# Fixed owners for two double banks of scores and maxima products in an attention and expert kernel

## The chip, the cores and the metric

The kernel runs on one core of one Trainium2 chip. The metric is the device time of one execution in microseconds (us), lower is better. TensorE multiplies matrices into PSUM, a small accumulation memory of eight banks of 2 KB per partition; VectorE, ScalarE and GpSimd work beside it, and SyncE issues transfers. In profiles they are called PE, DVE, ACT, POOL and SP.

## The reference, cut to what matters

Three layers follow each other. Attention comes first, for 2 batches of 8 heads, 768 positions and head size 64. Each query and each key gets a hash bucket of 6 bits, and a query sees only keys of its own bucket. Then comes a dense gated layer, then a layer of 8 experts with one expert per token.

```
mask = q_bucket[:, :, :, None] == k_bucket[:, :, None, :]
scores = scale * np.matmul(q, k.transpose(0, 1, 3, 2))
scores = np.where(mask, scores, -1000000000.0)
scores = scores - np.max(scores, axis=-1, keepdims=True)
attn = np.exp(scores)
attn = attn / (np.sum(attn, axis=-1, keepdims=True) + 1e-09)
attn_out = np.matmul(attn, v)
# dense layer
a = x @ w1;  b = x @ w2;  h = a * b @ w3;  x = h @ w_out
# experts
e_idx = np.argmax(x @ w_gate + modality_bias[modality_id], axis=1)
out[mask] = gate_w[mask, None] * (np.maximum(x[mask] @ w1[e], 0.0) @ w2[e])
```

## The kernel before, in words

Attention runs over eight head pairs of 768 positions. The work is cut into units, twelve for a pair. A **maxima** unit (`stage_1`, L336) multiplies 128 queries of one head with all 768 keys, two matmuls of 384 columns (L341) into a double bank of PSUM; VectorE then takes the row maxima straight from there (L348, `tensor_reduce` into `nm`). After six units GpSimd and a transpose (`stage_f`, L357) turn the maxima into two extra rows of the query operand. A **scores** unit (`stage_2`, L369) multiplies 128 keys of both heads with 384 queries, four matmuls (L376) into a double bank; ScalarE takes the exponential from there into `pt` (L377), and GpSimd or, for one unit in six late on, VectorE adds the `pt` tiles up (L383). `stage_a` (L385) multiplies `pt` with the values (L391).

A loop over slots (L777) puts the units in order. Slot i issues maxima unit i (for i below 96 = `NU`) and scores unit i - 9 (for i from 9 = `LEAD` to 104). So slots 0 to 8 hold maxima only, 9 to 95 both, maxima first and scores last on TensorE, and 96 to 104 scores only. Names in the trace and the order tell the unit: `m7_4_1` is head pair 7, query tile 4, head 1, which is slot 93; `s7_0_0` of the same slot is pair 7, half 0, key tile 0. Below, "the reduction of slot 93" is that of its maxima, "the exponential of slot 93" that of its scores.

Between these units other work fills the slots. Pieces of the dense layer's weights are loaded and split into a high and a low part: until slot 86 (`SWITCH`) a piece takes three VectorE operations, a cast on ScalarE (L489) and a difference on GpSimd (L490); later the reloaded first weights take a cast on ScalarE (L489) and a difference on VectorE (L490), queued at the end of a slot (`flush`, L519), so behind that slot's exponential on ScalarE and behind its reduction on VectorE. Products of two weight matrices (L591) fill TensorE from slot 22 on. From slot 90 the input of the dense layer is split too (L633 cast, L635 difference), and from slot 95 the first products of that layer begin (`moe_half`, L669, matmuls L677). After attention the dense layer and the experts follow, TensorE almost without a pause.

Each engine works through its instructions in the order in which they are written; semaphores between engines are put in when the program is built. PSUM tiles come from a pool by a tag (`ps`, L195). The tags `m`, `w`, `u` and `a` have one bank each. The tag `s` has two double banks, and maxima and scores both ask for it. When a tile is asked for, the pool decides at build time which of the tag's two double banks it gets; the tile's first write then waits for the last reader of what lay there. That reader is VectorE's reduction if the bank held maxima, and ScalarE's exponential if it held scores.

Of the kernel before, what the change touches and what calls it, by code (L numbers as in the profile page):

```python
# [20 lines left out]
P = 128  # L21
# [19 lines left out]
LEAD = 9  # L41
# [122 lines left out]
def body(tc, qT, kT, vP, w1d, w2d, w3d, wod, mod, wgate, mbias, e1, e2, cst, out):  # L164
# [25 lines left out]

    pst = ExitStack()
    psum = [pst.enter_context(tc.tile_pool(name="psum1", bufs=1, space=PSUM))]
    nbuf = {"s": 2, "m": 1}

    def ps(tag, shape, name):  # L195
        return psum[0].tile(shape, F32, tag=tag, name=name, bufs=nbuf.get(tag, 1))
# [31 lines left out]
    NU = 2 * 6 * NPAIR  # L228
# [107 lines left out]
    def stage_1(u):  # L336
        p, qt, hd = u
        q, k = head_t[p, hd, "q"], head_t[p, hd, "k"]
        s = ps("s", [P, 2, 512], f"m{p}_{qt}_{hd}")
        for half in range(2):  # L340
            PE.matmul(  # L341
                s[:, half, 0:HS], q[0:KROWS[hd], 0, qt * P:qt * P + P], k[0:KROWS[hd], 0, half * HS:half * HS + HS],
                start=True, stop=True,
            )
        if qt % 3 == 0 and hd == 0:
            nm_t[p, qt // 3] = r_nm([P, 32])
        nm = nm_t[p, qt // 3]
        DVE.tensor_reduce(nm[:, 3 * hd + qt % 3:3 * hd + qt % 3 + 1], s[:, :, 0:HS], AX.XY, ALU.max, negate=True)  # L348
        if qt % 3 == 2 and hd == 1:
            v, fin = nm[:, 6:12], nm[:, 12:24].bitcast(F32R).rearrange("p (d x t) -> p d x t", d=2, x=2)  # L350
            v3 = v.rearrange("p (d t) -> p d t", d=2)
            POOL.tensor_scalar(v, nm[:, 0:6], C_MASK / 2, None, ALU.is_lt)
            POOL.tensor_mul(v, v, nm[:, 0:6])
            POOL.tensor_copy(fin[:, :, 0, :], v3)
            POOL.tensor_sub(fin[:, :, 1, :], v3, fin[:, :, 0, :].bitcast(F32))
# [12 lines left out]

    def stage_2(j):  # L369
        p, half, c = sunits[j]  # L370
        s = ps("s", [P, 2, 512], f"s{p}_{half}_{c}")
        cl = slice(half * HS, half * HS + HS)
        for hd in range(2):
            q, k = head_t[p, hd, "q"], head_t[p, hd, "k"]
            for i, n in enumerate((KROWS[hd], P)):
                PE.matmul(s[:, hd, 0:HS], k[0:n, i, c * P:c * P + P], q[0:n, i, cl], start=(i == 0), stop=(i == 1))  # L376
        ACT.activation(pts[j % NP][:, :, 0:HS], s[:, :, 0:HS], AF.Exp, scale=SCALE)  # L377
        if c == 1:
            acc_t[p, half] = r_acc([P, 2, HS + 1])
        if c:  # L380
            acc = acc_t[p, half]
            on_dve = c in next(cs_ for end, cs_ in ACC_DVE if j < end)
            (DVE if on_dve else POOL).tensor_add(acc, pts[(j - 1) % NP] if c == 1 else acc, pts[j % NP])  # L383
# [174 lines left out]
    slot = [0]  # L558
# [218 lines left out]
    for i in range(NU + LEAD + NLAG + 1):  # L777
# [46 lines left out]
        p, ph = divmod(i, 12)  # L824
# [3 lines left out]
        if i < NU:  # L828
            if p and ph == 9 and p + 3 < NPAIR:
                load_pair(p + 3)  # L830
            stage_1(units[i])
            fill()
            if long:
                fill()
# [30 lines left out]
        if 0 <= j < NU:  # L865
            if j % 12 == 3 and j // 12 + 1 < NPAIR:
                load_v(j // 12 + 1)
            if i == LEAD:
                busy(4, "m")
            stage_2(j)  # L870
            if not both:
                fill()
# [84 lines left out]
    nbuf = {"t": 2, "ab": 4}  # L957
# [582 lines left out]
```

## Time and profile before

| | us |
|---|---|
| median of 3 runs | 686.03 (685.93 to 688.89) |
| the profiled execution, its own time | 685.69 |
| span of that execution | 683.9 |
| TensorE busy | 651.8 (95%) |
| VectorE busy | 386.3 (56%) |
| ScalarE busy | 314.0 (46%) |
| GpSimd busy | 317.8 (46%) |

Busy shares are means over the whole span. Attention fills the first 300 us or so, and there VectorE and GpSimd are loaded heavily in places; from 300 to 600 us TensorE alone is close to 100%. TensorE's granted clock is the full one in nearly all of the span (mean 0.998). The difference between the span and the execution's own time is 1.8 us. A wait in the trace is idle time of an engine, put down to the instruction that ended it.

### The profile page before, as it was taken

The page shows a single profiled execution, that of the slowest core. Times are in us where ns is not written, and L with a number is a line of the kernel's source. Part 1 is how long each engine was busy: PE and PEld are TensorE (multiplying, and loading weights), DVE is VectorE, ACT ScalarE, POOL GpSimd, SP SyncE. Part 2 cuts the span into 40 slices and gives each one's busy share as a digit, 9 for nine tenths or more (in the row PEclk, how much of TensorE's full clock was granted, in tenths as well). Part 3 has the DMA queues.
Part 4 walks back from the last instruction along what each step waited for, and adds up shares of the span by engine and source line. Part 5 has one row for each costly group of instructions (what it writes and reads, how often), then busy time and mean ns, then how long its engine had stood idle before and what let it go on. Part 6 is the DMA issues. An engine that isn't in the chain of part 4 may idle for free. (4 is left out here: it accounts for less than half of the span.)

```text
span 683.9 us, 11034 instructions
## 1 busy us (share of the span) xinstructions
PE 651.8 (95%) x4038; PEld 511.9 (75%) x4038; DVE 386.3 (56%) x617; ACT 314.0 (46%) x534; POOL 317.8 (46%) x312
## 2 busy tenths in 40 slices
PE   7888999999999997999999999999999999999995
PEld 2544566666566754678989898989888899899984
DVE  6897676767586889642632121121275865575550
ACT  7264665556556556553422121221224665564551
POOL 7498888687858776552524233231214212111110
PEclk9999999999999999999999999999999999999999
DMA  8755555473736463303201010100036977766630
GB/s 225 239 187 171 186 150 199 120 234 112 223 111 205 137 203 108 105 20 96 65 16 47 16 47 16 47 1 32 1 121 221 333 267 238 238 205 212 209 115 19
DMA packets 41691, 94.04 MB, mean 138 GB/s; under 512 B 6352, under 2 KB 12032, under 8 KB 41632
## 3 DMA queue, kind: packets, MB, share of 16 engines
q1 hardware_dynamic: 39552, 86.72, 40.7%
q0 software_dynamic: 2080, 6.56, 2.8%
q8 instruction: 34, 0.56, 0.4%
q14 instruction: 25, 0.20, 0.1%
HBM read 72.98 MB, written 12.94 MB: 126 GB/s over the span
## 5 line engine op out<-in xcount | busy, mean ns | idle before, releaser
L677 PE MATMUL ab<-x,w 128*128 128x256 f32 x1152 | 143.6, 284 | 1.3 <-ACT rT L361 0.7
L677 PEld LDWEIGHTS ab<-x,w 128*128 128x128 f32 x1152 | 140.6, 191 | 5.6 <-ACT asb L685 2.1
L383 POOL TENSOR_TENSOR acc<-acc,pt 128x770 f32<-128x770 f32 x61 | 113.5, 1861 | 23.8 <-ACT pt L377 21.3
L348 DVE TENSOR_REDUCE nm<-m 128x1 f32<-128x768 f32 x96 | 91.4, 955 | 56.7 <-PE m L341 56.5
L377 ACT ACTIVATE pt<-s 128x768 f32<-128x768 f32 x96 | 78.0, 813 | 89.3 <-PE s L376 86.2
L376 PEld LDWEIGHTS s<-q,k 128*128 128x128 f32 (+1 forms) x384 | 63.9, 189 | 43.8 <-issue 23.2
L376 PE MATMUL s<-q,k 128*128 128x384 f32 (+1 forms) x384 | 91.5, 360 | 2.8 <-ACT pt L377 2.1
L688 POOL TENSOR_TENSOR g<-gf,g 128x256 fp32r<-128x256 f32 x48 | 35.6, 741 | 123.1 <-ACT g L687 119.8
L1206 DVE TENSOR_TENSOR eu<-er,eu 128x1024 fp32r<-128x1024 f32 x56 | 68.0, 1232 | 23.4 <-ACT eu L1205 21.6
L391 PE MATMUL a<-pt,v 128*64 128x385 f32 x384 | 76.4, 504 | 0.0
L686 DVE TENSOR_TENSOR gf<-asb,ab 128x256 f32<-128x256 f32 x48 | 20.2, 421 | 97.0 <-ACT asb L685 96.9
L1369 PE MATMUL e1F<-ex,eu 128*128 128x256 f32 x576 | 70.3, 283 | 0.5 <-DVE ex L1335 0.3
L1369 PEld LDWEIGHTS e1F<-ex,eu 128*128 128x128 f32 x576 | 69.7, 190 | 1.4 <-DVE ex L1335 0.5
L1395 POOL DMA_INDIRECT out<-o,sidx x13 | 13.7, 1051 | 122.3 <-ACT o L1394 106.2
L1387 PE MATMUL e2F<-eu,h 128*128 128x512 f32 x288 | 68.8, 394 | 0.0
L341 PE MATMUL m<-k,q 78*128 78x384 f32 x192 | 52.0, 353 | 11.1 <-ACT pt L377 5.7
L1387 PEld LDWEIGHTS e2F<-eu,h 128*128 128x128 f32 x288 | 53.3, 188 | 11.1
L1205 ACT CAST eu<-er 128x1024 fp32r<-128x1024 f32 x56 | 57.6, 1046 | 8.1 <-DMA er<-e 7.8
L1002 PE MATMUL x2p<-w,g 128*128 128x512 f32 x240 | 58.1, 396 | 0.0
L591 PE MATMUL w<-wo,w 128*128 128x512 f32 x192 | 51.4, 400 | 2.2 <-ACT ev L594 1.6
L1002 PEld LDWEIGHTS x2p<-w,g 128*128 128x128 f32 x240 | 44.2, 188 | 11.4 <-issue 2.1
L685 ACT COPY asb<-ab 128x256 f32<-128x256 f32 x48 | 17.9, 373 | 73.7 <-PE ab L677 73.7
(203 smaller groups left out, 800.1 us busy)
## 6 DMA issues: line engine op xcount, KB each, us to landing
er<-e SPq DMA_DIRECT2D x56, 512.0 KB
cr<-w3d SPq DMA_DIRECT2D x16, 512.0 KB
cr<-wod SPq DMA_DIRECT2D x8, 512.0 KB
cr<-w1d SPq DMA_DIRECT2D x8, 512.0 KB
wfd<-cT SPq DMA_DIRECT2D x16, 256.0 KB
cr<-w2d SPq DMA_DIRECT2D x8, 512.0 KB
st<-wfd SPq DMA_DIRECT2D x16, 256.0 KB
raw<-kT SPq DMA_DIRECT2D x8, 384.0 KB
```

The lines of the kernel that those rows point to most:

```text
L341: PE.matmul(s[:, half, 0:HS], q[0:KROWS[hd], 0, qt * P:qt * P + P], k[0:KROWS[hd], 0, half * HS:half * HS + HS], start=True, stop=True,)
L348: DVE.tensor_reduce(nm[:, 3 * hd + qt % 3:3 * hd + qt % 3 + 1], s[:, :, 0:HS], AX.XY, ALU.max, negate=True)
L376: PE.matmul(s[:, hd, 0:HS], k[0:n, i, c * P:c * P + P], q[0:n, i, cl], start=(i == 0), stop=(i == 1))
L377: ACT.activation(pts[j % NP][:, :, 0:HS], s[:, :, 0:HS], AF.Exp, scale=SCALE)
L383: (DVE if on_dve else POOL).tensor_add(acc, pts[(j - 1) % NP] if c == 1 else acc, pts[j % NP])
L391: PE.matmul(a_t[p, half][64 * hd:64 * hd + 64, :], v[:, c, 64 * hd:64 * hd + 64], pts[j % NP][:, hd, :], start=(c == 0), stop=(c == QT - 1 ...
L677: PE.matmul(ab[:, j, :], w12[j][:, st, c, fs], x[:, mv, c, :], start=(c == 0 and i == 0), stop=(c == 3 and i == 2))
L1002: PE.matmul(st["ps"], g_t[ch][:, a, f, i * P:i * P + P], w34[b][:, f, :], start=(f == 0 and k == 0), stop=(f == 7 and k == 2),)
L1205: ACT.copy(t[:, 0, sl], raw)
L1206: DVE.tensor_sub(t[:, 1, sl], raw, t[:, 0, sl].bitcast(F32))
L1369: PE.matmul(o[f], w[:, st, c, fs], x[:, mv, c, :], start=(c == 0 and i == 0), stop=(c == 3 and i == 2))
L1387: PE.matmul(o, h[:, st, f, sl], w[:, mv, f, :], start=(f == 0 and k == 0), stop=(f == 7 and k == 2))
```

## The change: what it does

The tag `s` shrinks to one double bank, and a new tag `x` gets the other one. The place in memory stays as it was: four single banks and two double banks. Maxima take `x` in all slots from 9 on; in slots 0 to 8 they take `s` in even slots and `x` in odd ones. Scores take `s`, and from slot 96 on `x` in even slots. `nbuf` for attention becomes empty, since one buffer is the default.

```
-    nbuf = {"s": 2, "m": 1}
+    nbuf = {}
...
     def stage_1(u):
-        s = ps("s", [P, 2, 512], f"m{p}_{qt}_{hd}")
+        s = ps("sx"[slot[0] >= LEAD or slot[0] % 2], [P, 2, 512], f"m{p}_{qt}_{hd}")
...
     def stage_2(j):
-        s = ps("s", [P, 2, 512], f"s{p}_{half}_{c}")
+        s = ps("sx"[slot[0] >= NU and slot[0] % 2 == 0], [P, 2, 512], f"s{p}_{half}_{c}")
```

No instruction is added, removed or moved. What differs in the built program is which semaphores some of TensorE's matmuls wait for. The first place is TensorE in slots 21 and 22, the end of head pair 0's scores and the start of pair 1's (`m1_4_1` and `s1_0_0` are slot 21, `m1_5_0` is slot 22). A row is one matmul or several equal ones, with the engine whose semaphore it waits for; "Activation" is ScalarE, "DMAHW" a transfer.

```order
-L341 MATMUL m1_4_1_562<-k11_19_88,q11_17_86 128x384 [waits Activation_49]
+L341 MATMUL m1_4_1_562<-k11_19_88,q11_17_86 128x384 [waits DVE_49]
 L341 MATMUL m1_4_1_562<-k11_19_88,q11_17_86 128x384
 L391 MATMUL a0_1_455<-pt2_22_91,v_30_152 64x385 x2
-L376 MATMUL s1_0_0_569<-q01_16_85,k01_18_87 128x384 [waits DMAHW2_49,DVE_49]
+L376 MATMUL s1_0_0_569<-q01_16_85,k01_18_87 128x384 [waits DMAHW2_49,Activation_49]
 L376 MATMUL s1_0_0_569<-q01_16_85,k01_18_87 128x384
 L376 MATMUL s1_0_0_569<-q11_17_86,k11_19_88 128x384 [waits DMAHW3_49]
 L376 MATMUL s1_0_0_569<-q11_17_86,k11_19_88 128x384
-L341 MATMUL m1_5_0_584<-k01_18_87,q01_16_85 128x384 [waits Activation_49]
+L341 MATMUL m1_5_0_584<-k01_18_87,q01_16_85 128x384 [waits DVE_49]
 L341 MATMUL m1_5_0_584<-k01_18_87,q01_16_85 128x384
```

In slots 21 and 22 the maxima took the bank of the slot before's scores, and the scores the bank of the slot before's maxima; now each kind follows its own. In slots 23 to 90 the waits are the same before and after. The second place is TensorE in slots 91 and 93 to 95, the last maxima; shown are slot 93 (`m7_4_1`, `s7_0_0`) and the start of 94 (`m7_5_0`).

```order
-L341 MATMUL m7_4_1_2561<-k11_19_88,q11_17_86 128x384 [waits Activation_49]
+L341 MATMUL m7_4_1_2561<-k11_19_88,q11_17_86 128x384 [waits DVE_49]
 L341 MATMUL m7_4_1_2561<-k11_19_88,q11_17_86 128x384
 L391 MATMUL a6_1_2475<-pt2_22_91,v_191_2040 64x385 x2
-L376 MATMUL s7_0_0_2567<-q01_16_85,k01_18_87 128x384 [waits DMAHW2_49,DVE_49]
+L376 MATMUL s7_0_0_2567<-q01_16_85,k01_18_87 128x384 [waits DMAHW2_49,Activation_49]
 L376 MATMUL s7_0_0_2567<-q01_16_85,k01_18_87 128x384 [waits DMAHW7_49,DMAHW6_49]
 L376 MATMUL s7_0_0_2567<-q11_17_86,k11_19_88 128x384 [waits DMAHW3_49]
 L376 MATMUL s7_0_0_2567<-q11_17_86,k11_19_88 128x384
-L341 MATMUL m7_5_0_2583<-k01_18_87,q01_16_85 128x384 [waits Activation_49]
+L341 MATMUL m7_5_0_2583<-k01_18_87,q01_16_85 128x384 [waits DVE_49]
 L341 MATMUL m7_5_0_2583<-k01_18_87,q01_16_85 128x384
```

Slots 91 and 95 change in the same way; in slot 92 (`m7_4_0`) the waits stay. At slot 96 the first scores (`s7_0_3`) wait for VectorE instead of ScalarE. VectorE's own queue does not change; this is what stands in it, before and after, from the reduction of slot 90 (`m7_3_0`) to that of slot 93, `w0` and `w1` being the split weights of the dense layer and `st` the tiles they are reloaded into.

```order
L348 TENSOR_REDUCE nm_229_2495<-m7_3_0_2492 128x1 [waits PE_49]
L490 TENSOR_TENSOR w1_221_2412<-st_223_2415,w1_221_2412 128x512 [waits DMAHW4_49,Activation_49]
L348 TENSOR_REDUCE nm_229_2495<-m7_3_1_2512 128x1 [waits PE_49]
L490 TENSOR_TENSOR w0_220_2411<-st_224_2417,w0_220_2411 128x512 [waits DMAHW5_49,Activation_49]
L490 TENSOR_TENSOR w1_221_2412<-st_227_2487,w1_221_2412 128x512 [waits DMAHW6_49,Activation_49]
L635 TENSOR_TENSOR x_231_2510<-xT0_10_79,x_231_2510 128x256
L348 TENSOR_REDUCE nm_229_2495<-m7_4_0_2541 128x1 [waits PE_49]
L490 TENSOR_TENSOR w0_220_2411<-st_230_2508,w0_220_2411 128x512 [waits DMAHW1_49,Activation_49]
L635 TENSOR_TENSOR x_231_2510<-xT0_10_79,x_231_2510 128x256
L348 TENSOR_REDUCE nm_229_2495<-m7_4_1_2561 128x1 [waits PE_49]
```

Nothing moved here: between two reductions stand one or two splits, each of which waits for ScalarE's cast of the same piece.

## Rows read from the trace of the kernel before

**Rows 1.** The page, busy time, share of span and instructions by engine.

```profile
PE 651.8 (95%) x4038; PEld 511.9 (75%) x4038; DVE 386.3 (56%) x617; ACT 314.0 (46%) x534; POOL 317.8 (46%) x312
```

**Rows 2.** TensorE's waits: waiting instruction, releaser, us in total, times, longest.

```profile
PE m L341 <- ACT pt L377: 5.7, 6, 1.0
PE m L341 <- DVE nm L348: 4.9, 9, 0.9
```

**Rows 3.** Busy time by stretch: stretch, its us, busy us by engine, clock, DMA.

```profile
300.00:400.00 100.00, 99.42 (x732) 88.05 (x729) 32.32 (x74) 29.97 (x74) 34.36 (x41) 1.00 0.18 49
```

**Rows 4.** Timeline of TensorE, slots 21 and 22: start, duration, what, [idle before].

```profile
56.65 0.62 PE L341 MATMUL m<-k,q 128*128 128x384 f32 x2 [0.96 <-ACT pt L377]
...
59.93 0.61 PE L341 MATMUL m<-k,q 78*128 78x384 f32 x2 [0.96 <-ACT pt L377]
...
61.57 1.43 PE L591 MATMUL w<-wo,w 128*128 128x512 f32 x5 [0.56 <-POOL w L490]
```

**Rows 5.** Timeline of VectorE, the reductions of slots 20 and 21.

```profile
56.69 0.95 DVE L348 TENSOR_REDUCE nm<-m 128x1 f32<-128x768 f32 x1
...
59.60 0.95 DVE L348 TENSOR_REDUCE nm<-m 128x1 f32<-128x768 f32 x1
```

**Rows 6.** Timeline of TensorE, slots 91 to 95 and the next products.

```profile
262.17 0.62 PE L341 MATMUL m<-k,q 128*128 128x384 f32 x2 [0.96 <-ACT pt L377]
...
265.53 0.62 PE L341 MATMUL m<-k,q 78*128 78x384 f32 x2 [0.92 <-DVE nm L348]
...
266.87 0.97 PE L376 MATMUL s<-q,k 78*128 78x384 f32 x4
268.81 0.61 PE L341 MATMUL m<-k,q 128*128 128x384 f32 x2 [0.96 <-ACT pt L377]
...
270.15 0.97 PE L376 MATMUL s<-q,k 78*128 78x384 f32 x4
272.02 0.61 PE L341 MATMUL m<-k,q 78*128 78x384 f32 x2 [0.90 <-ACT pt L377]
...
275.30 0.62 PE L341 MATMUL m<-k,q 128*128 128x384 f32 x2 [0.96 <-ACT pt L377]
...
277.46 1.58 PE L677 MATMUL ab<-x,w 128*128 128x256 f32 x12
```

**Rows 7.** Timeline of VectorE, the reductions of slots 90 to 94 and two pairs of splits.

```profile
261.87 0.95 DVE L348 TENSOR_REDUCE nm<-m 128x1 f32<-128x768 f32 x1
...
264.53 0.94 DVE L348 TENSOR_REDUCE nm<-m 128x1 f32<-128x768 f32 x1
266.05 2.59 DVE L490 TENSOR_TENSOR w<-st,w 128x512 fp32r<-128x512 f32 x2 [0.58 <-ACT w L489]
...
268.90 0.94 DVE L348 TENSOR_REDUCE nm<-m 128x1 f32<-128x768 f32 x1
...
271.54 0.95 DVE L348 TENSOR_REDUCE nm<-m 128x1 f32<-128x768 f32 x1
272.51 1.29 DVE L490 TENSOR_TENSOR w<-st,w 128x512 fp32r<-128x512 f32 x2
...
274.05 0.95 DVE L348 TENSOR_REDUCE nm<-m 128x1 f32<-128x768 f32 x1
```

**Rows 8.** Timeline of ScalarE, exponentials of slots 91 and 93 and the casts behind them.

```profile
264.70 0.81 ACT L377 ACTIVATE pt<-s 128x768 f32<-128x768 f32 x1 [1.51 <-PE s L376]
265.40 1.13 ACT L489 CAST w<-st 128x512 fp32r<-128x512 f32 x2
...
271.16 0.81 ACT L377 ACTIVATE pt<-s 128x768 f32<-128x768 f32 x1 [1.59 <-PE s L376]
271.87 1.13 ACT L489 CAST w<-st 128x512 fp32r<-128x512 f32 x2
```

**Rows 9.** Timeline of GpSimd, the additions of slots 91 and 94.

```profile
265.65 1.83 POOL L383 TENSOR_TENSOR acc<-acc,pt 128x770 f32<-128x770 f32 x1 [1.60 <-ACT pt L377]
...
275.33 1.83 POOL L383 TENSOR_TENSOR acc<-pt,pt 128x770 f32<-128x770 f32 x1 [4.60 <-ACT pt L377]
```

## The prediction

> **What bounds the kernel now.** I read the page's busy times first, then whom TensorE waited for, then the order of the instructions with their waits, and last the timeline of each engine in the two stretches where that order differs. TensorE is busy 651.8 us of a span of 683.9 [rows 1], so a change counts only by the idle time of TensorE that it adds or takes away. Of that idle time the maxima products (L341) hold 5.7 us behind the exponentials (L377) and 4.9 us behind the reductions (L348) [rows 2]. Once attention is over TensorE hardly waits: from 300 to 400 us it is busy 99.42 of 100 us [rows 3]. So a shift at the end of attention reaches the end of the program in full, unless something late in attention takes it back.
>
> The order names the places. The other four engines have the same rows and the same waits before and after. TensorE has the same instructions, and other waits in slots 21 and 22, in 91 and 93 to 95, and a little at 96 to 98. In every other slot that holds both kinds each already keeps its own double bank. Where the kinds exchange banks, the maxima of slot i wait for the exponential of slot i-1, which reads the bank they take, and the scores of slot i for the reduction of slot i-1. With fixed owners the maxima wait for that reduction and the scores for that exponential. The six waits that make up the 5.7 us, each 0.90 to 0.96 us, are the two of slots 21 and 22 [rows 4] and the four of slots 91, 93, 94 and 95 [rows 6]. The change takes away precisely these. What counts is when the reductions end that take their place.
>
> **Slots 21 and 22.** The maxima of slot 21 start at 56.65 [rows 4]. VectorE begins the reduction of slot 20 only at 56.69 and ends it at 57.64; that of slot 21 runs from 59.60 to 60.55 [rows 5]. From the end of a reduction to the start of the matmul that waits for it I count 0.06 (264.53 + 0.94 to 265.53, rows 6 and 7). So slot 21 starts at 57.70, 1.05 later, and slot 22 at 60.61 instead of 59.93, 0.68 later. VectorE is not held up by that: its reduction of slot 21 starts at 59.60 behind other work, and its operand is there at 57.70 + 0.62. Behind the maxima of slot 22 stand two products of L591 and a third that waited 0.56 until 61.57 for a difference made on GpSimd. That difference hangs on conversions of VectorE that don't move. The third product is now ready 0.68 later against a wait of 0.56: 0.12 late at most, less if matmuls overlap their ends as the rows show them doing. I take +0.05. If that cover were gone it would be +0.68.
>
> **Slots 91 to 95.** VectorE is behind here, since it splits reloaded weights (L490) between the reductions. I follow it slot by slot, the row's present start behind "for".
> - Slot 91: the reduction of slot 90 ends at 261.87 + 0.95 = 262.82 [rows 7], so the maxima start at 262.88 for 262.17, +0.71 [rows 6].
> - Its scores and its exponential come 0.71 later, 265.41 for 264.70. In ScalarE's queue two casts of weights stand behind that exponential and start 0.70 after it [rows 8]. VectorE's next pair of splits sat idle 0.58 until the first cast was done, so it starts at 266.76 for 266.05, and the reduction of slot 92 at 269.61 for 268.90 [rows 7].
> - Slot 92 already waits for its reduction and keeps 265.53: its wait of 0.92 absorbs the shift of TensorE. The scores keep 266.87.
> - Slot 93: the reduction of slot 92 ends at 269.61 + 0.94 = 270.55, so the maxima start at 270.61 for 268.81, +1.80. Scores follow 1.34 later (268.81 to 270.15), the exponential 1.01 after that (270.15 to 271.16), the casts 0.71 after that: 273.67 for 271.87.
> - Slot 94 starts when TensorE is through with those scores, by 271.95 + 0.97 = 272.92 for 272.02. The reduction that it waits for needs no cast of slot 93 and ends near its present 272.49.
> - Slot 95: VectorE's next pair of splits now starts at 274.32, which is 273.67 + 0.61 for the cast + 0.04 of lag, for 272.51: +1.81. From the pair's start to the next reduction are 1.54 (272.51 to 274.05), so the reduction of slot 94 runs from 275.86 to 276.81. Slot 95 starts at 276.87 for 275.30, **+1.57**.
> - Behind it stand its scores and the first experts' products (L677, 277.46), all moved by the same amount. In slots 96 to 98 both banks are used in turn as before. The one new wait there, of the scores of slot 96 for the reduction of slot 95, is queued on TensorE behind all twelve products of L677 and more, while that reduction is queued behind one split. I cost it at nothing; without the cover of those products it would be at most the 0.95 us of the reduction.
>
> The sum: 0.05 + 1.57 = **+1.6 us**. On the profiled execution of 685.69 us that is 687.3. The median of the runs shown, 686.03, lies 0.34 above that execution, which gives 687.6. I say 687.5.
>
> **Bounds.** Below: if the replacing reductions cost nothing, all 5.7 us of [rows 2] go. Rows speak against that end, since the reduction of slot 90 ends at 262.82 whatever happens later, but it is the floor. Above: with nothing absorbed slots 21 and 22 cost 0.68; and if the pair of splits at 274.32 ran beside an addition of GpSimd, as the pair at 266.05 does, it would take 2.59 instead of 1.29 [rows 7, 9], which makes +1.57 into +2.87. Together +3.6. My value lies below the middle of the two because GpSimd has no addition between the exponentials of slots 92 and 94 (idle 4.60 before 275.33, rows 9).
>
> **Rivals.**
> - *The waits go and little replaces them: faster, down to 680.3 us on the median.* For it: the six waits are real, and the exponentials they name are what the change takes out of the way. Against: five of the six replacing reductions end after the start they replace, by 0.47 to 1.03 (57.64 against 56.65, 269.84 against 268.81, 272.49 against 272.02). It decides only where VectorE reached its reductions earlier than it does now. Chance 0.04.
> - *Only the first wait counts, ScalarE passes nothing on: no change.* If VectorE's splits didn't wait for casts, its reductions would stay where they are: slot 93 would start at 269.90, slot 94 at 272.55, slot 95 at 274.05 + 0.95 + 0.06 = 275.06 for 275.30, -0.24. With +0.05 that is 685.8 on the median. For it: VectorE is nearly always busy here. Against: its idle 0.58 ended by a cast, and the pair at 272.51, which starts just as its cast ends at 271.87 + 0.61 [rows 7, 8]. Chance 0.13.
> - *The additions of GpSimd slide onto the splits: slower by 2.9 to 3.6, 688.9 to 689.6.* Place: the pair at 274.32. It decides if an addition of GpSimd is running when that pair starts. For it: the pair at 266.05 overlaps the addition of 265.65 to 267.48 and takes twice the time of the one at 272.51, which overlaps none. Against: the 4.60 us in which GpSimd has nothing to add. Chance 0.13. [...]
> - *The bank assignment does nothing*, as the order in the timed program might not bear on any start. The order and the six waits by name speak against it. 686.0, chance 0.03.
> - The forecast, a shift of 1.0 to 2.3 us: 0.67.
>
> **How the numbers follow.** A difference of 0.5% is 3.4 us, about what a measurement of this kernel can tell from none. The forecast, the second rival and the fourth lie inside it, and most of the third, with run-to-run spread (one of the three runs shown is 688.89): same 0.86. Slower by more than 3.4 needs the top of the third or a spread on top of the forecast: 0.10. Faster by more than 3.4: 0.04. The range goes from a little below the no-change cases, 685.0, to the top of the third, 689.6.
>
> **What would show it.** Right: L341 no longer waits for L377 in slots 21, 22, 91 and 93 to 95. Its waits for L348 rise from 4.9 to about 13 us: 2.01 and 0.60 in slots 21 and 22 (60.61 less the end of the scores at 57.70 + 1.34 + 0.97), then 1.67, 0.22, 2.77, none and 1.90 in 91 to 95, less the present 0.92. VectorE idles some 1.3 us before the pair at 266.8 and 1.7 before the pair at 274.3, each ended by a cast. The first product of L677 starts near 279.0 instead of 277.46. Wrong: maxima of slot 91 before 262.8 or of slot 93 before 270 (the first rival); L677 at 277.5 or sooner (the second) or past 280 (the third); a shift at 279 that is gone by 300.

## The result, and the profile after

The changed kernel takes **692.26 us** (median of 5 runs, 690.85 to 693.22) against 686.03 for the kernel before (5 runs, 685.57 to 688.89). The ratio is 1.008, with a 95% interval of 1.0054 to 1.0106: slower, where a shift of 1.6 us had been forecast and 689.6 was the top of the range. A loss of more than 3.4 us had been given a chance of 0.10. The profiled execution took 691.16 us, with a span of 689.4.

The page's busy times and TensorE's waits of the changed kernel, for [rows 1, 2]:

```profile
PE 654.7 (95%) x4038; PEld 513.6 (75%) x4038; DVE 386.5 (56%) x617; ACT 313.8 (46%) x534; POOL 318.7 (46%) x312
```

```profile
PE m L341 <- DVE nm L348: 13.7, 14, 4.3
```

The waits of the maxima for the exponentials are gone, as the order said. Those for the reductions came to 13.7 us (about 13 forecast), but the longest is 4.3 us, and no wait of that length was in the forecast. TensorE is also busy 2.9 us longer with the same matmuls. Those are two different things, and the timelines show both. First TensorE in slots 21 and 22 of the changed kernel, which answers [rows 4]:

```profile
57.65 0.62 PE L341 MATMUL m<-k,q 128*128 128x384 f32 x2 [1.98 <-DVE nm L348]
...
60.59 0.62 PE L341 MATMUL m<-k,q 78*128 78x384 f32 x2 [0.63 <-DVE nm L348]
61.05 1.92 PE L591 MATMUL w<-wo,w 128*128 128x512 f32 x7
```

The starts are within 0.05 us of the forecast, and the wait for GpSimd at L591 is swallowed: seven products run through without it. The next scores start at 63.70 for 63.73. In this execution the early place costs nothing; under e1 stands one in which it does.

Now TensorE in slots 90 to 95, from the scores of slot 90, for [rows 6]. All of it lies 0.30 us later than before the change (scores of slot 90 at 260.54 for 260.24).

```profile
260.54 0.97 PE L376 MATMUL s<-q,k 78*128 78x384 f32 x4
263.17 0.62 PE L341 MATMUL m<-k,q 128*128 128x384 f32 x2 [1.66 <-DVE nm L348]
...
265.83 0.62 PE L341 MATMUL m<-k,q 78*128 78x384 f32 x2 [0.24 <-DVE nm L348]
...
267.18 0.97 PE L376 MATMUL s<-q,k 78*128 78x384 f32 x4
272.50 1.01 PE L341 MATMUL m<-k,q 128*128 128x384 f32 x2 [4.35 <-DVE nm L348]
...
274.92 1.65 PE L376 MATMUL s<-q,k 78*128 78x384 f32 x4
276.37 0.85 PE L341 MATMUL m<-k,q 78*128 78x384 f32 x2
...
280.51 0.62 PE L341 MATMUL m<-k,q 128*128 128x384 f32 x2 [0.85 <-DVE nm L348]
...
282.66 1.58 PE L677 MATMUL ab<-x,w 128*128 128x256 f32 x12
```

The waits of slots 91 and 92 are 1.66 and 0.24 us; 1.67 and 0.22 had been worked out. Slot 95 waits 0.85 instead of 1.90, because by then TensorE itself is late. So the total of 13.7 us is near the forecast by luck: slot 93 waits 4.35 instead of 2.77, and the two misses offset each other. From slot 93 to 279 the same matmuls take longer: 1.01 for the pair of maxima products (0.62 elsewhere after a wait), 1.65 for the scores (0.97). From the scores of slot 90 to the first L677 it takes 22.12 us, against 277.46 - 260.24 = 17.22 before.

What kept slot 93 is in VectorE's and GpSimd's timelines of the same stretch, for [rows 7, 9]:

```profile
264.83 0.94 DVE L348 TENSOR_REDUCE nm<-m 128x1 f32<-128x768 f32 x1
267.04 2.59 DVE L490 TENSOR_TENSOR w<-st,w 128x512 fp32r<-128x512 f32 x2 [1.26 <-ACT w L489]
269.55 2.02 DVE L635 TENSOR_TENSOR x<-xT,x 128x256 fp32r<-128x256 f32 x1
271.50 0.94 DVE L348 TENSOR_REDUCE nm<-m 128x1 f32<-128x768 f32 x1
...
277.96 1.29 DVE L490 TENSOR_TENSOR w<-st,w 128x512 fp32r<-128x512 f32 x2 [3.45 <-ACT w L489]
...
279.50 0.95 DVE L348 TENSOR_REDUCE nm<-m 128x1 f32<-128x768 f32 x1
```

```profile
266.64 1.84 POOL L383 TENSOR_TENSOR acc<-acc,pt 128x770 f32<-128x770 f32 x1 [2.28 <-ACT pt L377]
269.20 2.10 POOL L383 TENSOR_TENSOR acc<-acc,pt 128x770 f32<-128x770 f32 x1 [0.72 <-ACT pt L377]
```

The pair of splits starts 0.7 us later relative to the start of the stretch, as forecast (267.04 less 0.30). The small input difference behind it, L635, takes 2.02 us, where one in the clear takes 0.41 to 0.42. It begins at 269.55, after GpSimd's addition has begun at 269.20, and ends 0.27 us after that addition (271.57 against 271.30). The addition hangs on the exponential of slot 92, which did not move relative to the stretch; VectorE's work moved into it. Before the change the two stood like this, VectorE first:

```profile
268.56 0.41 DVE L635 TENSOR_TENSOR x<-xT,x 128x256 fp32r<-128x256 f32 x1
```

```profile
268.90 1.83 POOL L383 TENSOR_TENSOR acc<-acc,pt 128x770 f32<-128x770 f32 x1 [1.41 <-ACT pt L377]
```

L635 was only 0.34 us ahead of the addition, so a shift of 0.7 us puts it behind. There it took 2.02 us for 0.41. In e3 and e6 below three more L635 begin while an addition runs: they take 1.17, 1.59 and 1.18 us, and each ends 0.28 or 0.29 us after that addition.

The longer matmuls are the clock. TensorE by stretches in the changed kernel: stretch, its length, busy us and count, granted clock, DMA share, GB/s:

```profile
270.00:272.00 2.00, 0.00 (x0) 0.98 0.72 256
272.00:274.00 2.00, 1.50 (x4) 0.50 0.02 6
274.00:276.00 2.00, 2.00 (x7) 0.50 0.43 131
276.00:278.00 2.00, 2.00 (x8) 0.50 0.00 0
278.00:280.00 2.00, 1.65 (x8) 0.81 0.10 30
```

After an idle time of 4.35 us the granted clock, 1.00 until 271, stands at 0.50 from 272 for nearly 7 us (0.62 from 278 to 279, 1.00 from 279 on). Slot 93 pays for it on the path: from its maxima to its exponential it is 272.50 to 276.61, 4.11 us, against 268.81 to 271.16, 2.35 us before. ScalarE's rows show the exponential and the casts that VectorE then waits 3.45 us for:

```profile
276.61 0.81 ACT L377 ACTIVATE pt<-s 128x768 f32<-128x768 f32 x1 [6.74 <-PE s L376]
277.31 1.13 ACT L489 CAST w<-st 128x512 fp32r<-128x512 f32 x2
```

So the stretch adds up in this execution. The chain that had been forecast gives +1.57. The reduction of slot 92 starts at 271.50 - 0.30 = 271.20 instead of the forecast 269.61, which is +1.59. The clock is 4.11 - 2.35 = +1.76. Together 17.22 + 4.92 = 22.14, and 22.12 was measured. Of the 5.5 us between the two spans 4.9 lie here. The other 0.6 lie before slot 90 and after the first L677 and carry no wait that the change names.

### The profile page after: what moved, and what is told of

Same layout as the page of the kernel before. It is cut to its first block, busy times and chain, and to the rows that moved or that the text cites. A ratio compares the mean times of both kernels' runs of the same rounds, so it can differ in the third digit from the quotient of the medians.

```text
span 689.4 us, 11035 instructions
## 1 busy us (share of the span) xinstructions
PE 654.7 (95%) x4038; PEld 513.6 (75%) x4038; DVE 386.5 (56%) x617; ACT 313.8 (46%) x534; POOL 318.7 (46%) x312
## 5 line engine op out<-in xcount | busy, mean ns | idle before, releaser
L677 PE MATMUL ab<-x,w 128*128 128x256 f32 x1152 | 143.6, 284 | 1.3 <-ACT rT L361 0.7
L677 PEld LDWEIGHTS ab<-x,w 128*128 128x128 f32 x1152 | 140.6, 191 | 5.6 <-ACT asb L685 2.1
L391 PE MATMUL a<-pt,v 128*64 128x385 f32 x384 | 77.8, 512 | 0.0
L341 PE MATMUL m<-k,q 78*128 78x384 f32 x192 | 52.7, 357 | 13.9 <-DVE nm L348 13.7
L591 PE MATMUL w<-wo,w 128*128 128x512 f32 x192 | 51.3, 401 | 1.6 <-ACT ev L594 1.6
L383 POOL TENSOR_TENSOR acc<-pt,pt 128x770 f32<-128x770 f32 x16 | 29.6, 1849 | 48.4 <-ACT pt L377 46.5
```

What stands on the lines that cost most here:

```text
L341: PE.matmul(s[:, half, 0:HS], q[0:KROWS[hd], 0, qt * P:qt * P + P], k[0:KROWS[hd], 0, half * HS:half * HS + HS], start=True, stop=True,)
L391: PE.matmul(a_t[p, half][64 * hd:64 * hd + 64, :], v[:, c, 64 * hd:64 * hd + 64], pts[j % NP][:, hd, :], start=(c == 0), stop=(c == QT - 1 ...
L677: PE.matmul(ab[:, j, :], w12[j][:, st, c, fs], x[:, mv, c, :], start=(c == 0 and i == 0), stop=(c == 3 and i == 2))
```

## Experiments

Theory A: in slots 91 to 95 the maxima now wait for reductions that stand in VectorE's queue behind the weights' splits. The first such wait, 0.7 us longer than the one it replaces, passes over ScalarE's casts to VectorE, pushes L635 behind a GpSimd addition, and the long wait that follows, 4.35 us, lowers TensorE's granted clock to 0.50. The rivals stand in the expectations. Times are medians, with the ratio to the kernel before in the same job and its 95% interval.

The exchange of banks was rebuilt by slots with one helper: a slot in the tuple turns the two owners round from there on. The tuple (21, 22, 91, 93, 94, 95, 96) stands for the kernel before: e1 has its late part and e2 its early part, and their traces show that part's waits of 0.90 to 0.96 us again.

```
+    turned = lambda: sum(slot[0] >= t for t in SLOTS) % 2
-        s = ps("sx"[slot[0] >= LEAD or slot[0] % 2], ...)
+        s = ps("sx"[(slot[0] >= LEAD or slot[0] % 2) ^ turned()], ...)
-        s = ps("sx"[slot[0] >= NU and slot[0] % 2 == 0], ...)
+        s = ps("sx"[(slot[0] >= NU and slot[0] % 2 == 0) ^ turned()], ...)
```

**e1, the early place alone.** SLOTS = (91, 93, 94, 95, 96).

> Fixed owners in slots 21 and 22 alone; slots 91 to 96 exchange banks as before. Theory A (the whole loss is made in slots 91 to 95): as before, 686.0 within 1 us; TensorE's waits for the reductions in slots 21 and 22 are 2.0 and 0.6 us and the wait of 0.56 us for GpSimd at L591 is gone. Rival B (the early place takes part, through shifts of what follows): slower than before by 1.5 us or more.

Measured: 686.42 us (12 runs), ratio 1.0002 (0.9990 to 1.0013). In the median theory A holds and rival B falls. The profiled execution (687.68 us) shows that the early place isn't free in every execution, though. TensorE in slots 21 and 22:

```profile
57.69 0.62 PE L341 MATMUL m<-k,q 128*128 128x384 f32 x2 [1.97 <-DVE nm L348]
...
59.03 1.65 PE L376 MATMUL s<-q,k 78*128 78x384 f32 x4
60.60 1.01 PE L341 MATMUL m<-k,q 78*128 78x384 f32 x2
```

The same wait of 2 us is followed here by slower matmuls (1.65 for the scores, 0.97 in the changed kernel) and a lower clock (0.99 in the mean from 20 to 258 us, 1.00 before the change), and the stretch of slot 90 begins at 262.07 instead of 260.24, 1.83 us later. In the changed kernel's profile the clock did not fall there (1.00 from 50 to 66). The median doesn't show the price, and the kernel before is not free of such executions either: 8 of its 21 in this job took 687.0 to 688.0 us at a mean clock of 0.994 to 0.996, where the profiled one had 0.998. Where the clock fell in those is not traced.

**e2, the late place alone.** SLOTS = (21, 22).

> Fixed owners from slot 23 on; slots 21 and 22 exchange banks as before. Theory A: as the changed kernel, 691 to 693 us, with L677 first at about 282.7 and a wait of 4.3 us before the maxima of slot 93. Rival B: some us faster than the changed kernel. A further rival, that the loss hangs on the 0.3 us by which the late place lies later in the changed kernel's trace: near 687.5, as the prediction had it.

Measured: 691.57 us (6 runs), ratio 1.0073 (1.0058 to 1.0088). The wait before slot 93 is 4.37 us in its trace, the stretch begins at 260.24 as before the change, and the loss is there: theory A holds, and the 0.3 us of offset are not the cause. The first L677 starts at 284.06, since the clock stays low here until about 284 (0.50 from 272 to 284, 0.84 from 284 to 286): the stretch takes 23.82 us where the changed kernel's took 22.12.

**e3, L635 behind the reduction.** Two lines move.

```
-        if 0 <= i - SWITCH - NSTEP < HP + 2:
-            norm_step(0, i - SWITCH - NSTEP)
...
             stage_1(units[i])
             fill()
             if long:
                 fill()
+        if 0 <= i - SWITCH - NSTEP < HP + 2:
+            norm_step(0, i - SWITCH - NSTEP)
```

> Fixed owners everywhere; the input's splits of slots 90 to 95 (L633, L635, norm_step) are issued behind the maxima of their slot instead of ahead of them, so that on VectorE L635 stands behind the reduction of slot 92 and not ahead of it. Theory A (L635 fell behind a GpSimd addition, 2.02 us instead of 0.41, and the wait of 4.35 us it lengthened let TensorE's clock fall): the reduction of slot 92 starts as the pair of splits ends, the maxima of slot 93 near 270.5 instead of 272.5; with the clock still at its upper level the time is 688 to 689, with the clock fallen all the same 690. Rival C (the wait before slot 93 comes from ScalarE's casts alone): no change, 691 to 693.

Measured: 690.53 us (10 runs, 687.33 to 695.31), ratio 1.0066 (1.0040 to 1.0092). Its TensorE starts slot 93 so, with the scores of slot 90 at 262.00:

```profile
272.03 0.62 PE L341 MATMUL m<-k,q 128*128 128x384 f32 x2 [2.42 <-DVE nm L348]
```

That is 10.03 us after those scores, against 11.96 in the changed kernel: the 4.35 fell to 2.42, close to the 2.77 that the prediction had without the collision. So L635 behind the addition made the difference, and rival C falls. It falls by the trace and not by the time, whose interval overlaps that of the changed kernel (1.0054 to 1.0106). The single executions spread over 8 us, and the shortest have the highest mean clock: 687.33 and 687.36 at 0.997, 688.82 at 0.995, and the other seven, 689.41 to 695.31, between 0.984 and 0.992. In the profiled one, 689.41 at 0.992, the clock stays at 1.00 from slot 90 to the first L677. It fell in slot 21, behind a wait of 2.00 us (0.50 from 59 to 65, 0.99 in the mean from 20 to 258), and the scores of slot 90 start at 262.00, as late as in e1 (262.07). Where it fell in the slower ones is not traced.

**e4 and e5, TensorE kept busy.** e4 puts ten products ahead of slot 93; e5 five there, and two ahead of slot 95.

```
+        if i in (93, 95):
+            busy({93: 5, 95: 2}[i], "m")
         if i < NU:
```

> Fixed owners everywhere; ten products of the identity (L331, 0.34 us each) are put on TensorE ahead of the maxima of slot 93, into a bank that nothing reads. They should end before the reduction that those maxima wait for. Theory A: the maxima of slot 93 start at 272.5 as in the changed kernel, the granted clock stays near 1.00 from 272 to 279 us, and the time falls by 1.7 us, to about 690.5. Rival D (the slow matmuls after the wait are a cold start of the pipeline, not the clock, or the clock falls for another reason): no gain.

> The run before with the right size: one product of the identity is recorded as two matmuls and took 0.66 us, so ten of them outlasted the wait. Now five (3.3 us) stand ahead of the maxima of slot 93 and two (1.3 us) ahead of those of slot 95, fixed owners everywhere, nothing else changed. Theory A: the maxima of slot 93 start when their reduction ends, about 12 us after the scores of slot 90 start (272.50 against 260.54 in the changed kernel); the granted clock stays near 1.00; from the scores of slot 90 to the first L677 it takes 20.4 us instead of 22.1, and the time falls by about 1.7 us and spreads less. Rival D (the clock is not what costs): 22 us, no gain.

Measured: e4 692.92 us (6 runs), ratio 1.0089 (1.0073 to 1.0106); e5 690.51 us (5 runs, 689.40 to 690.94), ratio 1.0055 (1.0041 to 1.0069). In e4 the filling was too long: it ran 6.61 us and itself put off slot 93. From slot 90 the clock held at 1.00 until 282 and then fell, after a wait of 1.88 us before slot 95 (0.65 from 282 to 284, 0.50 from 284 to 286). e4 says nothing about the price. In e5 it ended in time. TensorE's timeline of e5, and its clock ahead of the filling and behind it:

```profile
268.63 3.39 PE L331 MATMUL busy<-ident 128*128 128x384 f32 x10
...
273.55 0.62 PE L341 MATMUL m<-k,q 128*128 128x384 f32 x2 [1.54 <-DVE nm L348]
```

```profile
264.00:266.00 2.00, 2.00 (x7) 0.50 0.86 244
266.00:268.00 2.00, 2.00 (x9) 0.81 0.71 154
268.00:272.00 4.00, 4.00 (x14) 1.00 0.19 59
272.00:274.00 2.00, 0.46 (x3) 1.00 0.29 92
274.00:282.00 8.00, 7.40 (x34) 1.00 0.33 113
```

Behind the filling the maxima take 0.62 us again and the clock stays at 1.00. The wait in front of them is now only 1.54 us, so this alone doesn't exclude a cold start behind a long wait (rival D). Against that speak the changed kernel, where matmuls stay slow for nearly 7 us and as long as the granted clock is 0.50, and e11 below, where the pair right behind a wait of 2.07 us takes 0.62 us and the slow ones begin later, with the clock (0.99 from 270 to 272; scores of 1.49 us from 271.74, at 0.50 from 272 to 274). In e1 above too the pair behind the wait takes 0.62 us, and the scores behind it 1.65. In this execution of e5 the clock had already fallen behind the wait of slot 91, and the stretch takes 21.79 us, hardly less than 22.12, where 20.4 were expected. The median is 1.75 us below the changed kernel's, as expected, while the two intervals overlap: the size of the clock's share is supported, not settled, by this run.

**e11, one exchange put back in slot 91.** SLOTS = (91,), and nothing else.

> The changed kernel with one exchange of banks put back, in slot 91 alone, so that its maxima start 0.7 us earlier, behind the exponential; all else as changed, no order touched. Theory A (that first 0.71 us pushes VectorE's pair of splits, and with it L635 of slot 92, behind a GpSimd addition that does not move; the long wait then costs clock): the pair starts as before the change, L635 takes 0.41 us and ends before the addition, the reduction of slot 92 ends 7.7 us after the maxima of slot 91 start, the wait before slot 93 is about 2.1 us instead of 4.35, and from the scores of slot 90 to the first L677 it takes about 18.1 us (17.2 before, 22.1 changed): the time is 687 to 688 where the clock stays up. Rival F (each slot's own reduction costs what it costs, no push): only the 0.7 us come back, 691.5.

Measured: 688.62 us (10 runs, 686.88 to 690.64), ratio 1.0031 (1.0018 to 1.0044). TensorE at slots 91 and 93, then VectorE, then GpSimd in e11:

```profile
262.66 0.62 PE L341 MATMUL m<-k,q 128*128 128x384 f32 x2 [0.96 <-ACT pt L377]
...
270.39 0.62 PE L341 MATMUL m<-k,q 128*128 128x384 f32 x2 [2.07 <-DVE nm L348]
```

```profile
269.05 0.41 DVE L635 TENSOR_TENSOR x<-xT,x 128x256 fp32r<-128x256 f32 x1
```

```profile
269.37 1.82 POOL L383 TENSOR_TENSOR acc<-acc,pt 128x770 f32<-128x770 f32 x1 [1.39 <-ACT pt L377]
```

L635 starts 0.32 us ahead of the addition and takes its 0.41; slot 93 starts 270.39 - 262.66 = 7.73 us after slot 91 and waits 2.07. The stretch takes 279.32 - 260.73 = 18.59 us, where 18.1 were expected: the clock still falls behind the wait of 2.07 (0.50 from 272 to 275). The execution with the highest mean clock, 0.998, took 686.88. Rival F (691.5) falls, and the interval lies below the changed kernel's. Giving back 0.7 us in one slot gave back 3.6 us of the 6.2 (692.26 to 688.62, in two jobs whose medians of before are 686.03 and 686.43).

**e6 and e7, the splits behind the next slot's maxima.** Besides the lines of e3:

```
-        flush()
+        if i < SWITCH:
+            flush()
...
+        if i >= SWITCH:
+            flush()
         fi = i if i <= 6 else i - 1
```

e6 has fixed owners; e7 has SLOTS = (21, 22, 91, 93, 94, 95, 96).

> Fixed owners; from slot 86 on the casts and differences of the reloaded weights (L489, L490) and the input's splits (L633, L635) are issued in the next slot, behind its maxima: on VectorE the reduction of a slot then stands ahead of the differences whose casts wait behind the exponential of the slot before. Theory A (the loss comes from reductions queued behind those differences, over ScalarE): the waits of 1.7, 2.8 to 4.4 and 0.9 to 1.9 us in slots 91 to 95 fall below 0.5 us each, the stretch from the scores of slot 90 to the first L677 takes 13 to 14.5 us instead of 17.2 before the change, and the time is 682.5 to 684, below both kernels. Rival E (a double bank for each kind is too little by itself, whatever VectorE's order): near 691.

> The same order of the splits, with the exchange of banks in slots 21, 22, 91 and 93 to 96 as before the change. Theory A: the exchange costs its four waits for the exponential, 0.9 to 1.0 us each in slots 91 to 95, so 686 give or take 1, and slower than with fixed owners by 2 to 4 us: the sign of the change turns with VectorE's order. Rival E: faster than with fixed owners, as before the change.

Measured: e6 686.41 us (11 runs), ratio 1.0005 (0.9989 to 1.0021); e7 686.75 us (11 runs), ratio 1.0003 (0.9993 to 1.0013). The loss of the fixed owners is gone once their reductions no longer stand behind splits that wait for the last exponential, so rival E falls. A gain of 2 to 4 us over the exchange was expected too and did not come. TensorE in e6 shows why:

```profile
262.98 0.62 PE L341 MATMUL m<-k,q 128*128 128x384 f32 x2 [1.65 <-DVE nm L348]
...
264.43 1.55 PE L376 MATMUL s<-q,k 78*128 78x384 f32 x4
...
268.86 0.51 PE L341 MATMUL m<-k,q 128*128 128x384 f32 x2
...
276.06 1.35 PE L677 MATMUL ab<-x,w 128*128 128x256 f32 x10
278.57 0.50 PE L677 MATMUL ab<-x,w 128*128 128x256 f32 x2 [1.16 <-DVE x L635]
```

Slot 93 no longer waits at all. But the wait of 1.65 us before slot 91 stays, and in this execution the clock falls behind it (0.86 in the mean from 258 to 270, scores of 1.55 us). A new wait of 1.16 us comes in at the dense layer's first products (L677), since their last input difference now stands behind the last reduction, and that behind a product of the second chunk's input (L641) that takes 2.07 us beside a GpSimd addition. The stretch takes 276.06 - 260.35 = 15.71 us, where 13 to 14.5 were expected.

**e8, e9 and e10, a version that beats both.** e8 is e6 with RATE2 = 1.2. e9 and e10 also start the second chunk's norm_0 steps two slots later; e9 has SLOTS = (91,), e10 fixed owners throughout.

```
-RATE2 = 1.4
+RATE2 = 1.2
...
-            if i == at + 4:
+            if i == at + 4 + 2 * ch:
```

> The order of the splits as in the last two, fixed owners, and the reloaded weights taken up at 1.2 instead of 1.4 pieces a slot (RATE2), so that fewer differences fall between slots 89 and 95. Theory A: as fast as with 1.4 or up to 1 us faster, if a wait is left there. If the weights come late instead, a wait of L677 for L490 takes its place in slots 95 to 104 and it is slower.

> Built on e8 (fixed owners, splits issued behind the next slot's maxima, 1.2 pieces a slot). Two waits were left there: 1.64 us before the maxima of slot 91, and 1.20 us of the first L677 for the last L635, which a product of the second chunk's input (L641) held up beside a GpSimd addition. So the second chunk's norm_0 steps begin two slots later (slot 96), and the banks are exchanged in slot 91 alone, where the exponential ends before the reduction. Theory A: the wait before slot 91 is 0.96 us instead of 1.64 and that of L677 below 0.3, the clock falls less often, and the time is 683 to 684.5, below both kernels. Rival: the waits move on to another engine's backlog in slots 92 to 95, no gain over e8 (685.8).

> The same without the exchange in slot 91: fixed owners in every slot. Theory A: 1.64 us before slot 91 as in e8, L677 without its wait, about 0.7 us and whatever the clock gives back slower than the run before; 684 to 685.5. Rival: equal to it, if slot 91's wait is made up in slot 92.

Measured: e8 685.79 us (11 runs), ratio 0.9989 (0.9976 to 1.0003); e9 **684.13 us** (5 runs, 683.46 to 686.49), ratio 0.9951 (0.9935 to 0.9968); e10 685.48 us (12 runs, 682.98 to 687.06), ratio 0.9977 (0.9964 to 0.9990). TensorE in e9:

```profile
264.73 0.62 PE L341 MATMUL m<-k,q 128*128 128x384 f32 x2 [0.96 <-ACT pt L377]
...
279.47 0.50 PE L677 MATMUL ab<-x,w 128*128 128x256 f32 x2 [0.88 <-DVE x L635]
```

e8 can't be told from the kernel before; e9 is faster than both kernels, and e10 is faster than the kernel before by less. In e9 the wait of slot 91 is the 0.96 us of the exponential, after which the clock stayed at 1.00 from 262 to 278; in e10 it is 1.65, and the clock stood at 0.50 from 266 to 269 behind it. The profiled execution of e9 is nevertheless its slowest, 686.49: its clock fell in slot 21 (0.50 from 60 to 65). The wait of L677 for L635 was expected below 0.3 in e9 and is still 0.88; in e10 none is recorded. e9 and e10 differ by the exchange in slot 91 alone, where the exponential is done before the reduction. Their medians lie 1.35 us apart, but the ends of their intervals meet (0.9968 and 0.9964), and e9 has five executions. So a mixed ownership is likely the best with this order, and not settled; the exchange in all its old slots was not run with it.

## Why the prediction was wrong

- *Where the change acts.* Right: slots 21 and 22 and 91 to 95, by the order; e1 and e2 show that the late place alone makes the loss in the median.
- *Slots 21 and 22, +0.05.* Right in the starts (57.65 and 60.59 for 57.70 and 60.61) and in the cover by L591; e1 adds that in some executions the clock falls there, which no term covers. That it did not in the profiled execution is luck.
- *Slot 91, +0.71, passed over ScalarE to the pair of splits.* Right: 1.66 and 0.24 us of wait, pair at 267.04 - 0.30 = 266.74 for 266.76.
- ***"the reduction of slot 92 at 269.61"* is the step that failed.** It moved the pair of splits and L635 together by 0.71 and let L635 keep its 0.41 us. The same paragraph said that the scores of slot 92 keep 266.87. So its exponential and GpSimd's addition behind that keep their place as well, and VectorE's moved work runs into an addition that stands still, from a lead of only 0.34 us. L635 took 2.02 us for the 0.41 it was given, which cost 1.59 us on the path. e3 and e11 show it in two different ways: one puts L635 behind the reduction, the other lets it start ahead of the addition.
- *The third rival* named the mechanism, additions that meet VectorE's differences, and gave it 0.13. It put it at the pair of 274.32, where GpSimd had nothing to add; the meeting came ahead of the reduction of slot 92 and not of slot 94, with a smaller operation.
- ***The clock* is a second term that failed: it was in no step and no rival.** The sum took every matmul at the duration that it had before, though it worked out a wait of 2.77 us before slot 93 where the longest of these slots had been 0.96. It cost 1.76 us in the profiled execution, and more in that of e2, where it stayed at 0.50 until about 284. The traces show it falling behind waits (4.35 us in the changed kernel, 2.07 in e11, 1.65 in e10), and not behind each of them (2.42 us in e3); what it costs in the mean over executions stays open.
- *Slot 95, +1.57.* Its own chain is right: pair, reduction, maxima, L677 follow each other as worked out (277.96, 279.50, 280.51, 282.66), only from a start that came 1.59 + 1.76 us late.
- *ScalarE passes nothing on* (the second rival) falls by VectorE's idle times of 1.26 and 3.45 us, each ended by a cast.
- The median lies 6.2 us above, the profiled execution 5.5. Two of the five executions took 692.98 and 693.22 us at a mean clock of 0.987 and 0.986, the others 690.85 to 692.26 at 0.992. Where the clock fell a second time in those two is not traced. A fall in slot 21 would fit: an estimate from e1 adds its 1.83 us to 691.16 and gives 693.0, and takes 0.005 off the mean clock (0.993 in e1's profile for 0.998 before).

## What to carry to other kernels

When a wait moves one engine's work, lay it against the work of the other engines that does not move. Here the collision came from the difference of two shifts, 0.7 us on VectorE and none on GpSimd, whose share the wait of slot 92 had absorbed, over a lead of 0.34 us; L635 took 2.02 us for 0.41. Who should own a bank is a question for each slot, by whose last reader ends first: one exchange put back in slot 91 gave back more than half of what the fixed owners had lost (e11). A wait on TensorE that grows to a few microseconds should also be priced with slower matmuls behind it: behind the 4.35 us here the granted clock stood at 0.50, and slot 93 took 4.11 us from its maxima to its exponential for 2.35; behind 2.42 us in e3 the clock stayed at 1.00.

## What the runs showed of the hardware that was not expected

- TensorE's granted clock went to 0.50 behind an idle time of 4.35 us for nearly 7 us in the changed kernel, and it also went there behind much shorter waits, in some profiles and not in others. Behind the wait of about 2.0 us in slot 21 it fell in six of ten profiles (e1, e3, e4, e5, e9 and e10, not in the changed kernel, e6, e8 and e11): the mean from 20 to 258 us is 0.99 in those six and 1.00 in the changed kernel, e6 and e8, and e11 has 1.00 from 50 to 66. Behind the wait of about 1.65 us in slot 91 it fell in four of eight (e5, e6, e8 and e10, not in the changed kernel, e2, e3 and e4): the mean from 258 to 270 is 0.86 in those four and 1.00 in the others. Behind 2.42 us before slot 93 of e3 it did not fall (1.00 from 270 to 290). So here the same wait cost clock in one execution and not in another.
- It fell behind waits below 1 us as well. In e7, whose banks are exchanged in slots 21 and 22 as before the change, the clock stood at 0.50 from 62 to 65, behind waits of 0.96, 0.96 and 0.55 us (0.99 in the mean from 20 to 258). The kernel before and e2 have nearly the same three waits, and their clock stayed at 1.00. The row behind the third wait took 1.43 us before ([rows 4]), and in e7

```profile
61.40 2.18 PE L591 MATMUL w<-wo,w 128*128 128x512 f32 x5 [0.55 <-POOL w L490]
```

- Times spread with the clock: e3 ranges over 8 us, from 687.33 at a mean clock of 0.997 to 695.31 at 0.987. e7, whose waits in slots 21, 22 and 91 to 95 all stay below 1 us, ranges over 1.8 us. That the waits make the difference is likely, and not shown by these two, which differ in VectorE's order too.
